# Attention's hash projections as fp32 products of the loaded rows, four quarters of the array in one call

## The chip, the cores and the metric

The kernel runs on one core of one Trainium2 chip. The metric is the device time of one execution in microseconds. Before the change the median of three runs is 671.51 us (669.77 to 671.78).

## What is computed

Three layers follow each other: bucketed attention, a mixture of experts with a capacity, and a second mixture of experts with a skip. The change touches the attention alone. Its reference, cut to what matters:

```python
q_bits = (np.einsum('bhsd,dk->bhsk', q, proj) > 0)
k_bits = (np.einsum('bhsd,dk->bhsk', k, proj) > 0)
mask = q_bucket[:, :, :, None] == k_bucket[:, :, None, :]
scores = np.where(mask, scale * np.matmul(q, k.transpose(0, 1, 3, 2)), -1000000000.0)
```

Batch 2, 8 heads, 768 positions, head dimension 64, 6 hash bits. Everything is float32.

## The kernel before, in words

**Units.** Attention is cut into 16 units of work: a batch, a pair of heads and one half of the 768 query positions. Each unit has six score tiles of 128 queries by 768 keys, one in each of six *slots*. There are 16 groups of keys, one for each batch and head; a unit uses two groups, and the first eight units use each pair of groups twice.

**How a score is made.** The loaded rows hold each head's 64 dimensions twice, on partitions 0 to 63 and 64 to 127 (qT and kT are laid out so). `splitq` and `splitk` (lines 143 to 158) cut them into a high part in fp32r and a rest: `Q1` and `K1` of 128 partitions, `Q2` and `K2` of 76. The score is the sum of two fp32r products (lines 199 and 201). Partitions 64 to 75 of `Q2` and `K2` hold the hash: 12 rows, six bits and six complements, 0 or 1 for queries and 0 or -BIG for keys, so that a pair in different buckets falls far below.

**The projections.** These 12 rows are what `projq` and `projk` make (lines 170 to 185): products of the signed projection matrix with the split rows, two fp32r products for each block of 384 positions (lines 172 and 173 for queries, 181 and 182 for keys), into a PSUM tile, and an eviction by VectorE that compares with a threshold (lines 175 and 184). `project` (line 160) does one or two of them in one PSUM tile `aux`, of which there is one buffer, shared with `fin`; where it does two, the second is put into partitions 32 to 43 by a projection matrix with 32 columns of zeros in front. There are 32 query and 32 key projections. The matrix is split in `signs` (line 72).

**The order.** Everything is issued in an order written out by hand, lines 327 to 445. For each slot (u, i) the kernel issues the score and its row maximum (VectorE, lines 203 to 205), the splits that are planned for the slot, at slot 1 the loads for later units, two products of attention and values (`av`, line 235, fp32, one head in each half of the columns), steps of the router's counting (`gens`, from unit 9 on), the projections planned for the slot (line 389), transposes of an older exponential (line 221), and the exponential of this slot on ScalarE (line 212). At slot 0 of unit 3 and later come the three products `fin` of a unit three before (line 278). The plan: query projections of the next unit at slots 2 and 3, those of a first K group at slots 4 and 5, those of a second K group at slot 5 and at slot 1 of the next unit. Units 0 to 4 and 9 split one K group each, units 5 to 8 two, units 10 to 15 none. Loads of kT, qT and v are issued from SP's queue; kT has three buffers, qT four. Scores have two PSUM buffers, so a score waits for the exponential two slots before.

**Start.** Before the first slot the kernel loads, splits group 0 and the first query block, projects them, then splits group 1 and the second query block (lines 331 to 342).

**After attention** come the two mixtures. At line 1248 their router makes four fp32 products of 192 columns, each with 32 columns of the array, side by side in one PSUM tile; the code before the change has no product that sets 64 rows of the array against the other 64.

```python
nc.tensor.matmul(s4[32 * d:32 * d + 32, :], self.wsg[:, d, :], yT[:, d, :],
                 start=True, stop=True, tile_position=(0, 32 * d))
```

Of the kernel before, what the change touches and what calls it, by code (L numbers as in the profile page):

```python
# [7 lines left out]
F32 = mybir.dt.float32  # L8
F32R = mybir.dt.float32r
# [4 lines left out]
ALU = mybir.AluOpType  # L14
# [4 lines left out]
BIG = 2.0 ** 33  # L19
# [4 lines left out]
class Net:  # L24
# [17 lines left out]
    def consts(self):  # L42
        nc = self.nc
        c = self.c = self.ctx.enter_context(self.pool("consts", 1))

        self.rows = ExitStack()
        x = self.x = self.rows.enter_context(self.pool("xp", 1))
        self.warm = x.tile([1, 1], F32, name="warm")
        nc.vector.memset(self.warm, 0.0)
        nc.scalar.activation(self.warm, self.warm, AF.Exp)  # L50
        self.zero = c.tile([128, 256], BF, name="zero")
        nc.vector.memset(self.zero, 0.0)
        jp = self.jp = x.tile([128, 128], I32, name="jp")
        nc.gpsimd.iota(jp, pattern=[[1, 128]], base=0, channel_multiplier=-1)

        ri = x.tile([12, 1], I32, name="ri")
        nc.gpsimd.iota(ri, pattern=[[0, 1]], base=0, channel_multiplier=1)
        thr = self.thr = x.tile([12, 2], F32, name="thr")
        nc.vector.tensor_scalar(thr[:, 0:1], ri, 5.5, -TINY, op0=ALU.is_gt, op1=ALU.mult)
        nc.vector.tensor_scalar(thr[:, 1:2], ri, 5.5, -TINY, op0=ALU.is_lt, op1=ALU.mult)  # L60

        sg = x.tile([128, 2, 12], F32, name="sg")
        nc.vector.memset(sg[:, 0, 0:6], 1.0)
        nc.vector.memset(sg[:, 0, 6:12], -1.0)
        nc.vector.memset(sg[:, 1, 0:6], -1.0)
        nc.vector.memset(sg[:, 1, 6:12], 1.0)

        prs = x.tile([128, 2, 76], F32, name="prs")
        nc.vector.memset(prs, 0.0)
        self.sg, self.prs = sg, prs  # L70

    def signs(self):

        nc, x, sg, prs = self.nc, self.x, self.sg, self.prs
        pr = x.tile([128, 12], F32, name="pr")
        nc.sync.dma_start(pr, self.A["proj"])
        nc.vector.tensor_tensor(prs[:, :, 32:44], sg, pr[:, None, :].to_broadcast([128, 2, 12]), op=ALU.mult)
        ph = x.tile([128, 2, 76], F32R, name="ph")
        nc.vector.tensor_copy(ph, prs)
        pl = x.tile([128, 2, 76], F32R, name="pl")  # L80
        nc.vector.tensor_tensor(pl, prs, ph.bitcast(F32), op=ALU.subtract)

        pk = x.tile([128, 76], F32R, name="pk")
        nc.vector.tensor_copy(pk[0:64], prs[0:64, 1, :])
        nc.vector.tensor_tensor(pk[64:128], prs[64:128, 1, :], ph[64:128, 1, :].bitcast(F32), op=ALU.subtract)
        self.ph, self.pl, self.pk = ph, pl, pk

    def ident(self):
        self.idf = self.c.tile([128, 128], F32, name="idf")
# [14 lines left out]
    def attention(self, r, later):  # L104

        nc, A = self.nc, self.A
        with self.rows as ctx:
# [44 lines left out]
            def splitq(u, a, eng=nc.gpsimd, ceng=nc.vector):  # L152
                d = UD[u]
                Q1 = d["Q1", a] = st.tile([128, 384], F32R, name="Q1")
                Q2 = d["Q2", a] = st.tile([76, 384], F32R, name="Q2")
                copy(ceng, Q1, d["q", a])
                eng.tensor_tensor(Q1[64:128], d["q", a][64:128], Q1[64:128].bitcast(F32), op=ALU.subtract)  # L157
                copy(ceng, Q2[0:64], d["q", a][0:64])

            def project(fs, tag="aux"):  # L160

                p = ps.tile([44, 384], F32, name="aux", tag=tag, bufs=1 if tag == "aux" else 2)

                k = len(fs)
                gs = [f(x, y, p[0:12 + 32 * i], slice(32 - 32 * i, 44), (i == k - 1, True)) for i, (f, x, y) in enumerate(fs)][::-1]
                for _ in range(2):
                    for g in gs:
                        next(g)

            def projq(u, a, p, c, ends):  # L170
                d = UD[u]
                nc.tensor.matmul(p, self.ph[:, 0, c], d["Q1", a], start=ends[0], stop=False, skip_group_check=True)
                nc.tensor.matmul(p, self.pl[:, 0, c], d["Q1", a], start=False, stop=ends[1], skip_group_check=True)
                yield
                nc.vector.tensor_scalar(d["Q2", a][64:76], p[32 - c.start:44 - c.start], self.thr[:, 0:1], None, op0=ALU.is_gt)
                yield

            def projk(g, j, p, c, ends):
                d = KH[g]
                sl = slice(j * 384, (j + 1) * 384)  # L180
                nc.tensor.matmul(p, self.pk[:, c], d["K1"][:, sl], start=ends[0], stop=False, skip_group_check=True)
                nc.tensor.matmul(p, self.ph[0:64, 1, c], d["K2"][0:64, sl], start=False, stop=ends[1], skip_group_check=True)
                yield
                nc.vector.tensor_scalar(d["K2"][64:76, sl], p[32 - c.start:44 - c.start], self.thr[:, 1:2], -BIG, op0=ALU.is_gt, op1=ALU.mult)
                yield

            def score(u, i):
# [148 lines left out]
            splitq(0, 0, nc.vector, nc.scalar)  # L336
            for g in range(2):
                loadv(g)
            project([(projk, 0, 0), (projk, 0, 1)], "pT")
            project([(projq, 0, 0)])  # L340
            splitk(1, nc.gpsimd, nc.scalar)
            splitq(0, 1, nc.vector, nc.scalar)
            loadk(order[0])
            loadv(order[0])
            loadq(1)
# [2 lines left out]
            for u in range(NU):  # L348
                if u + 1 < NU:
                    for a in range(2):  # L350
                        splits.setdefault((u, a), []).append((splitq, u + 1, a))
                        projs.setdefault((u, 2 + a), []).append((projq, u + 1, a))
                for x, g in enumerate(kplan.get(u, [])):
                    splits.setdefault((u, 2 + x), []).append((splitk, g))
                    for j in range(2):
                        at = (u, 4 + j) if x == 0 else ((u, 5), (u + 1, 1))[j]
                        projs.setdefault(at, []).append((projk, g, j))
            gens, full = [], [None]
            setup = {(0, 2): self.ident, (1, 3): self.consts2, (2, 3): later, (4, 3): r.consts2}
            projs[0, 0] = [(projk, 1, 0)]  # L360
            projs[0, 1] = [(projk, 1, 1)]
            projs[0, 2].append((projq, 0, 1))
            for u in range(NU):
                for i in range(6):
                    g = u * 6 + i
                    score(u, i)
                    if (u, i) in setup:
                        setup[u, i]()
                    for f, *x in splits.get((u, i), []):
                        f(*x, ceng=nc.scalar if u == 0 else nc.vector)  # L370
                    if i == 1:
                        if u + 2 < NU:
                            loadq(u + 2)
                        for _ in kplan.get(u + 1, []):
                            if nload < len(order):
                                loadk(order[nload])
                                loadv(order[nload])
                                nload += 1
                    ua, ca = (u - 1, i - 4) if i >= 4 else (u - 2, i + 2)
                    if ua >= 0:  # L380
                        av(ua, ca)

                    if i and gens and (i == 1 or u == NU - 1 or not full[0]):
                        full[0] = next(gens[0], self)
                        if full[0] is self:
                            gens.pop(0)
                            full[0] = None
                    if (u, i) in projs:
                        project(projs[u, i])

                    gp = g - 4 if g % 2 == 0 else g - 5
                    if gp >= 0:
                        tu, ti = divmod(gp, 6)
                        for cp in ((0, 1) if g % 2 == 0 else (2,)):
                            tpose(tu, ti // 2, cp)
                            if cp == 0:
                                expo(u, i)
                    if gp < 0 or g % 2:
                        expo(u, i)
                    if i == 0 and u >= 3:  # L400
                        fin(u - 3)
                        if u - 3 in (6, 7, 11):
                            q = 3 * (6, 7, 11).index(u - 3)
                            gens.append(r.count0(q, q + 3, sm, ps, ("pT", 2, "aux")))
# [1317 lines left out]
```

## Time and profile before

| | |
|---|---|
| median of three runs | 671.51 us |
| lowest and highest | 669.77, 671.78 us |
| profiled execution | 671.69 us |
| its span in the trace | 669.9 us |
| mean granted TensorE clock | 0.957 of full speed |
| TensorE busy | 621.7 us, 93% of the span |
| VectorE busy | 489.5 us, 73% |
| ScalarE busy | 398.9 us, 60% |
| GpSimd busy | 159.2 us, 24% |

All durations below come from the one profiled execution, whose time lies 0.2 us above the median. PE is TensorE, PEld its weight loads, DVE is VectorE, ACT is ScalarE, POOL is GpSimd, SP is the engine whose queue issues most loads. "L181" is line 181 of the kernel. Matmuls are pipelined: the duration of one contains latency that lies beside the next, so the cost of a matmul to the engine is read from one start to the next start. "busy tenths" and PEclk are given for 40 equal slices of the span, each about 16.7 us.

### The profile page before, as it was taken

How to read it: one execution, taken by the hardware profiler on the slowest of the kernel's cores; microseconds unless marked ns; L12 is line 12 of the kernel's file. 1: busy time of each engine (PE TensorE's matmuls, PEld its weight loads, DVE VectorE, ACT ScalarE, POOL GpSimd, SP SyncE). 2: the span in 40 equal slices, each digit the busy share in tenths (PEclk: the TensorE clock that was granted, in tenths of full speed). 3: DMA queues.
4: the chain of work that ended last, by engine and by line, in shares of the span. 5: the costliest groups of instructions: out<-in, count | busy, mean ns of one | idle time of the engine just before them, and what ended most of it. 6: DMA issues, size and time to landing. Idle time of an engine off the chain costs nothing.

```text
span 669.9 us, 11398 instructions
## 1 busy us (share of the span) xinstructions
PE 621.7 (93%) x3781; PEld 435.4 (65%) x3781; DVE 489.5 (73%) x1547; ACT 398.9 (60%) x909; POOL 159.2 (24%) x212
## 2 busy tenths in 40 slices
PE   7999999999999999956888899999999999999992
PEld 4666566655566666745747586686787778777781
DVE  7887788888877777475858776867633567999981
ACT  5677766666577777521525555554554557987870
POOL 2244233333111110142012130321502322211200
PEclk7799999999999999958988999999999999999996
DMA  6215212222111010035357828557665379999600
GB/s 199 96 38 160 74 41 79 89 92 72 48 63 34 0 49 2 2 132 193 127 157 292 253 53 281 169 174 256 217 219 191 111 263 363 388 381 326 231 22 13
DMA packets 53239, 99.69 MB, mean 149 GB/s; under 512 B 6421, under 2 KB 12949, under 8 KB 53168
## 3 DMA queue, kind: packets, MB, share of 16 engines
q1 hardware_dynamic: 42016, 76.21, 34.0%
q10 hardware_dynamic: 7072, 13.63, 5.9%
q0 software_dynamic: 4080, 8.99, 4.1%
q8 instruction: 34, 0.56, 0.3%
q14 instruction: 37, 0.30, 0.1%
HBM read 88.72 MB, written 12.46 MB: 151 GB/s over the span
## 4 chain that ended last, share of the span: by engine, by line
PE 73%; DVE 16%; DMA 3%; issue 3%; ACT 2%; POOL 1%; SPq 0%; ACTq 0%; POOLq 0%; DVEq 0%
PE av L235 10%; PE ph L1172 10%; PE pT L221 10%; PE y L1197 6%; PE S L201 5%; PE S L199 4%; DVE wlo L1359 4%; PE y L1203 4%; PE py L1419 2%; PE ph L1417 2%; PE ph L1419 2%; PE py L1418 2%; PE ph L1418 2%; PE py L1417 2%; PE fin L278 1%
## 5 line engine op out<-in xcount | busy, mean ns | idle before, releaser
L1359 DVE TENSOR_TENSOR wlo<-w,whi 128x512 fp32r<-128x512 f32 x192 | 123.6, 685 | 25.2 <-ACT whi L1358 22.8
L224 ACT ACTIVATE PT<-pT 128x512 f32<-128x512 f32 x135 | 80.3, 596 | 70.9 <-PE pT L221 70.8
L203 DVE TENSOR_REDUCE nm<-S 128x1 f32<-128x768 f32 x96 | 91.9, 957 | 31.3 <-PE S L201 29.1
L1358 ACT ACTIVATE whi<-w 128x512 fp32r<-128x512 f32 x192 | 109.4, 622 | 0.4 <-issue 0.4
L1172 PE MATMUL ph<-xT,w 128*128 128x192 f32 x512 | 104.8, 349 | 4.2 <-PEq L1517 4.2
L212 ACT ACTIVATE P<-S,b,g 128x768 f32<-128x768 f32 x96 | 94.8, 987 | 6.4 <-DVE b L205 6.4
L1172 PEld LDWEIGHTS ph<-xT,w 128*128 128x128 f32 x512 | 85.4, 198 | 14.4 <-issue 9.7
L221 PE MATMUL pT<-idf,P 128*128 128x128 f32 x576 | 83.3, 281 | 0.4 <-ACT PT L227 0.3
L221 PEld LDWEIGHTS pT<-idf,P 128*128 128x128 f32 x576 | 64.4, 142 | 29.4 <-issue 17.5
L235 PE MATMUL av<-PT,vd 128*64 128x384 f32 x360 | 77.5, 511 | 0.0
L157 POOL TENSOR_TENSOR Q<-qd,Q 64x384 fp32r<-64x384 f32 x30 | 31.1, 1038 | 144.3 <-PE pT L221 87.4
L199 PE MATMUL S<-K,Q 128*128 128x512 f32 x192 | 59.2, 390 | 0.7 <-ACT P L212 0.5
L1177 ACT ACTIVATE h<-ph 128x128 f32<-128x128 f32 x64 | 17.7, 277 | 61.2 <-PE ph L1172 34.2
L201 PE MATMUL S<-K,Q 76*128 76x512 f32 x192 | 51.5, 350 | 0.7 <-ACT Q L139 0.7
L201 PEld LDWEIGHTS S<-K,Q 76*128 76x128 f32 x192 | 30.6, 196 | 6.0 <-ACT K L139 1.2
L150 POOL TENSOR_TENSOR K<-kd,K 64x768 fp32r<-64x768 f32 x15 | 27.3, 1822 | 26.1 <-DVE K L141 12.2
L1203 PE MATMUL y<-w,h 128*64 128x512 f32 x128 | 32.9, 620 | 0.0
L235 PEld LDWEIGHTS av<-PT,vd 128*64 128x64 f32 x360 | 18.0, 134 | 22.7 <-issue 19.2
L199 PEld LDWEIGHTS S<-K,Q 128*128 128x128 f32 x192 | 30.8, 199 | 2.5 <-ACT P L212 1.7
L1320 POOL DMA_INDIRECT tb<-rec,ii x16 | 16.7, 1043 | 65.0 <-DVE cnt L1317 47.9
L1419 PE MATMUL py<-whi,hl 128*128 128x512 f32 x72 | 29.3, 406 | 1.4 <-DVE hl L1428 1.4
L1417 PE MATMUL py<-whi,hh 128*128 128x512 f32 x72 | 29.9, 416 | 0.0
(383 smaller groups left out, 1129.4 us busy)
## 6 DMA issues: line engine op xcount, KB each, us to landing
w<-w SPq DMA_DIRECT2D x28, 1024.0 KB
w<-u SPq DMA_DIRECT2D x26, 1024.0 KB
kd<-kT SPq DMA_DIRECT2D x16, 384.0 KB
qd<-qT SPq DMA_DIRECT2D x32, 192.0 KB
w<-u ACTq DMA_DIRECT2D x6, 1024.0 KB
w<-w ACTq DMA_DIRECT2D x4, 1024.0 KB
xd<-X SPq DMA_DIRECT2D x4, 780.0 KB
vd<-v SPq DMA_DIRECT2D x16, 192.0 KB
```

Source lines behind the costliest of these rows:

```text
L199: nc.tensor.matmul(S[:, n0:n1], d["Q1", a][:, ts], kd["K1"][:, n0:n1], start=True, stop=False)
L201: nc.tensor.matmul(S[:, n0:n1], d["Q2", a][:, ts], kd["K2"][:, n0:n1], start=False, stop=True)
L203: nc.vector.tensor_reduce(d["nm"][:, c], S, op=ALU.max, axis=AX.X, negate=True)
L212: nc.scalar.activation(P, S, AF.Exp, bias=d["b"][:, c], scale=d["g"][:, c], accum_out=d["s"][:, c])
L221: nc.tensor.transpose(p[:, a, b, :], d["P"][2 * ip + b][:, (2 * cp + a) * 128:(2 * cp + a + 1) * 128], self.idf)
L224: nc.scalar.activation(dst, p.rearrange("p a b q -> p a (b q)"), AF.Copy)
L235: nc.tensor.matmul(d["av"][64 * a:64 * a + 64, :], VH[b * 8 + 2 * p + a][:, c, :], d["PT"][:, c, a * 384:(a + 1) * 384], start=(c == 0), s ...
L1172: nc.tensor.matmul(ph, w1[f // 4][:, d, f % 4 * 128:f % 4 * 128 + 128], xT[:, d, :], start=(d == 0), stop=(d == 3))
L1203: nc.tensor.matmul(y2[64 * h:64 * h + 64, :], h2[:, 4 * h + f, :], res["w2"][h][:, f, :], start=(f == 0), stop=(f == 3))
L1358: nc.scalar.activation(hi[:, c, :], w[:, c, :], AF.Copy)
L1359: nc.vector.tensor_tensor(lo[:, c, :], w[:, c, :], hi[:, c, :].bitcast(F32), op=ALU.subtract)
L1417: nc.tensor.matmul(out, a[0][:, i, :], hi[:, i % 4, :], start=start, stop=False)
```

## The change

The signed projection matrix is no longer split; it stays in fp32 with 12 columns for queries and 12 for keys. Each projection is one fp32 product of it with the loaded rows (`d["q", a]` and `d["k"]`, not their splits). Product i of a call uses 64 rows of the array, the lower or the upper half in turn, and the 32 columns from 32 i, and writes PSUM partitions 32 i to 32 i + 11. A call takes up to four products; the evictions of the first two follow it, those of the other two come in the next slot. The plan is other: both query projections of the next unit and both of a first K group are one call at slot 3; both of a second K group are one call at slot 1 of the next unit; group 1 is one call at slot 0 of unit 0. Before the first slot, the second query block is split ahead of the projections, and all four projections of group 0 and unit 0 are one call.

```diff
--- before.py
+++ after.py
@@ -64,26 +64,15 @@
         nc.vector.memset(sg[:, 0, 6:12], -1.0)
         nc.vector.memset(sg[:, 1, 0:6], -1.0)
         nc.vector.memset(sg[:, 1, 6:12], 1.0)
-
-        prs = x.tile([128, 2, 76], F32, name="prs")
-        nc.vector.memset(prs, 0.0)
-        self.sg, self.prs = sg, prs
+        self.sg = sg
 
     def signs(self):
 
-        nc, x, sg, prs = self.nc, self.x, self.sg, self.prs
+        nc, x = self.nc, self.x
         pr = x.tile([128, 12], F32, name="pr")
         nc.sync.dma_start(pr, self.A["proj"])
-        nc.vector.tensor_tensor(prs[:, :, 32:44], sg, pr[:, None, :].to_broadcast([128, 2, 12]), op=ALU.mult)
-        ph = x.tile([128, 2, 76], F32R, name="ph")
-        nc.vector.tensor_copy(ph, prs)
-        pl = x.tile([128, 2, 76], F32R, name="pl")
-        nc.vector.tensor_tensor(pl, prs, ph.bitcast(F32), op=ALU.subtract)
-
-        pk = x.tile([128, 76], F32R, name="pk")
-        nc.vector.tensor_copy(pk[0:64], prs[0:64, 1, :])
-        nc.vector.tensor_tensor(pk[64:128], prs[64:128, 1, :], ph[64:128, 1, :].bitcast(F32), op=ALU.subtract)
-        self.ph, self.pl, self.pk = ph, pl, pk
+        self.prs = x.tile([128, 2, 12], F32, name="prs")
+        nc.vector.tensor_tensor(self.prs, self.sg, pr[:, None, :].to_broadcast([128, 2, 12]), op=ALU.mult)
 
     def ident(self):
         self.idf = self.c.tile([128, 128], F32, name="idf")
@@ -159,29 +148,32 @@
 
             def project(fs, tag="aux"):
 
-                p = ps.tile([44, 384], F32, name="aux", tag=tag, bufs=1 if tag == "aux" else 2)
-
-                k = len(fs)
-                gs = [f(x, y, p[0:12 + 32 * i], slice(32 - 32 * i, 44), (i == k - 1, True)) for i, (f, x, y) in enumerate(fs)][::-1]
-                for _ in range(2):
-                    for g in gs:
-                        next(g)
-
-            def projq(u, a, p, c, ends):
+                p = ps.tile([128, 384], F32, name="aux", tag=tag, bufs=1 if tag == "aux" else 2)
+                gs = [f(x, y, p[32 * i:32 * i + 12], i) for i, (f, x, y) in enumerate(fs)]
+                for g in gs:
+                    next(g)
+                for i, g in enumerate(gs):
+                    next(g)
+                    if i == 1:
+                        yield
+
+            def quarter(p, i, which, a):
+                r = 64 * (i % 2)
+                nc.tensor.matmul(p, self.prs[r:r + 64, which, :], a[r:r + 64], start=True, stop=True, tile_position=(r, 32 * i))
+
+            def projq(u, a, p, i):
                 d = UD[u]
-                nc.tensor.matmul(p, self.ph[:, 0, c], d["Q1", a], start=ends[0], stop=False, skip_group_check=True)
-                nc.tensor.matmul(p, self.pl[:, 0, c], d["Q1", a], start=False, stop=ends[1], skip_group_check=True)
+                quarter(p, i, 0, d["q", a])
                 yield
-                nc.vector.tensor_scalar(d["Q2", a][64:76], p[32 - c.start:44 - c.start], self.thr[:, 0:1], None, op0=ALU.is_gt)
+                nc.vector.tensor_scalar(d["Q2", a][64:76], p, self.thr[:, 0:1], None, op0=ALU.is_gt)
                 yield
 
-            def projk(g, j, p, c, ends):
+            def projk(g, j, p, i):
                 d = KH[g]
                 sl = slice(j * 384, (j + 1) * 384)
-                nc.tensor.matmul(p, self.pk[:, c], d["K1"][:, sl], start=ends[0], stop=False, skip_group_check=True)
-                nc.tensor.matmul(p, self.ph[0:64, 1, c], d["K2"][0:64, sl], start=False, stop=ends[1], skip_group_check=True)
+                quarter(p, i, 1, d["k"][:, sl])
                 yield
-                nc.vector.tensor_scalar(d["K2"][64:76, sl], p[32 - c.start:44 - c.start], self.thr[:, 1:2], -BIG, op0=ALU.is_gt, op1=ALU.mult)
+                nc.vector.tensor_scalar(d["K2"][64:76, sl], p, self.thr[:, 1:2], -BIG, op0=ALU.is_gt, op1=ALU.mult)
                 yield
 
             def score(u, i):
@@ -336,10 +328,10 @@
             splitq(0, 0, nc.vector, nc.scalar)
             for g in range(2):
                 loadv(g)
-            project([(projk, 0, 0), (projk, 0, 1)], "pT")
-            project([(projq, 0, 0)])
+            splitq(0, 1, nc.vector, nc.scalar)
+            for _ in project([(projk, 0, 0), (projk, 0, 1), (projq, 0, 0), (projq, 0, 1)]):
+                pass
             splitk(1, nc.gpsimd, nc.scalar)
-            splitq(0, 1, nc.vector, nc.scalar)
             loadk(order[0])
             loadv(order[0])
             loadq(1)
@@ -349,17 +341,15 @@
                 if u + 1 < NU:
                     for a in range(2):
                         splits.setdefault((u, a), []).append((splitq, u + 1, a))
-                        projs.setdefault((u, 2 + a), []).append((projq, u + 1, a))
+                        projs.setdefault((u, 3), []).append((projq, u + 1, a))
                 for x, g in enumerate(kplan.get(u, [])):
                     splits.setdefault((u, 2 + x), []).append((splitk, g))
                     for j in range(2):
-                        at = (u, 4 + j) if x == 0 else ((u, 5), (u + 1, 1))[j]
-                        projs.setdefault(at, []).append((projk, g, j))
+                        projs.setdefault((u, 3) if x == 0 else (u + 1, 1), []).append((projk, g, j))
             gens, full = [], [None]
             setup = {(0, 2): self.ident, (1, 3): self.consts2, (2, 3): later, (4, 3): r.consts2}
-            projs[0, 0] = [(projk, 1, 0)]
-            projs[0, 1] = [(projk, 1, 1)]
-            projs[0, 2].append((projq, 0, 1))
+            projs[0, 0] = [(projk, 1, 0), (projk, 1, 1)]
+            left = None
             for u in range(NU):
                 for i in range(6):
                     g = u * 6 + i
@@ -385,8 +375,12 @@
                         if full[0] is self:
                             gens.pop(0)
                             full[0] = None
+                    if left:
+                        next(left, None)
+                        left = None
                     if (u, i) in projs:
-                        project(projs[u, i])
+                        left = project(projs[u, i])
+                        next(left, None)
 
                     gp = g - 4 if g % 2 == 0 else g - 5
                     if gp >= 0:
```

## Rows read from the trace of the kernel before

**Rows 1.** The page: busy time and share of TensorE; granted clock in 40 slices.

```profile
PE 621.7 (93%) x3781; PEld 435.4 (65%) x3781; DVE 489.5 (73%) x1547; ACT 398.9 (60%) x909; POOL 159.2 (24%) x212
...
PEclk7799999999999999958988999999999999999996
```

**Rows 2.** Busy time in two stretches: length, PE, PEld, DVE, ACT, POOL, clock, DMA.

```profile
0.00:20.00 20.00, 16.02 (x53) 9.20 (x54) 14.71 (x36) 10.77 (x20) 6.17 (x10) 0.69 0.69 224
120.00:160.00 40.00, 40.00 (x236) 23.63 (x234) 32.70 (x78) 25.66 (x52) 12.56 (x13) 1.00 0.19 58
```

**Rows 3.** The chain that ended last: `fin` at slot 0, start and duration.

```profile
58.08 0.74 PE fin L278 x6
74.34 0.74 PE fin L278 x6
...
142.32 0.74 PE fin L278 x6
159.71 0.74 PE fin L278 x6
178.44 0.74 PE fin L278 x6
194.51 0.74 PE fin L278 x6
209.69 0.74 PE fin L278 x6
```

**Rows 4.** Timeline of TensorE, 102 to 113 us: start, duration, line, operation.

```profile
103.21 0.37 PE L181 MATMUL aux<-K,pk 128*44 128x384 f32 x1
...
104.36 0.66 PE L221 MATMUL pT<-idf,P 128*128 128x128 f32 x4
...
109.71 0.34 PE L181 MATMUL aux<-K,pk 128*12 128x384 f32 x1
109.98 0.34 PE L182 MATMUL aux<-K,ph 64*12 64x384 f32 x1
110.25 0.66 PE L221 MATMUL pT<-idf,P 128*128 128x128 f32 x4
...
111.54 0.87 PE L235 MATMUL av<-PT,vd 128*64 128x384 f32 x4
112.34 0.35 PE L172 MATMUL aux<-Q,ph 128*12 128x384 f32 x1
...
112.70 0.49 PE L221 MATMUL pT<-idf,P 128*128 128x128 f32 x3
```

**Rows 5.** Timeline of TensorE at a router product, line 1248, and the next.

```profile
350.94 0.53 PE L1248 MATMUL s<-yT,wsg 128*32 128x192 f32 x8
351.41 0.59 PE L1172 MATMUL ph<-xT,w 128*128 128x192 f32 x2
```

**Rows 6.** Timeline of TensorE in unit 9; in brackets idle time and releaser.

```profile
168.80 0.34 PE L172 MATMUL aux<-Q,ph 128*12 128x384 f32 x1 [1.00 <-DVE Q L175]
```

**Rows 7.** Timeline of all engines at the start; first scores of units 0, 1, 2.

```profile
5.24 0.94 ACT L139 ACTIVATE Q<-qd 128x384 fp32r<-128x384 f32 x2 [0.30 <-DMA qd<-qT]
...
7.84 0.84 PE L199 MATMUL S<-K,Q 128*128 128x512 f32 x2
...
9.39 1.87 DVE L157 TENSOR_TENSOR Q<-qd,Q 64x384 fp32r<-64x384 f32 x1 [0.18 <-ACT Q L139]
...
11.29 0.96 DVE L203 TENSOR_REDUCE nm<-S 128x1 f32<-128x768 f32 x1
...
25.93 0.59 PE L199 MATMUL S<-K,Q 128*128 128x512 f32 x2
...
39.80 0.60 PE L199 MATMUL S<-K,Q 128*128 128x512 f32 x2
```

**Rows 8.** Groups by line and shape, 0 to 240 us: count, busy us, mean ns.

```profile
L184 DVE TENSOR_SCALAR K<-aux,thr 12x384 fp32r<-12x384 f32 x32 | 19.5, 608 | 3.6 <-PE aux L182 2.8
L175 DVE TENSOR_SCALAR Q<-aux,thr 12x384 fp32r<-12x384 f32 x30 | 18.2, 608 | 1.0
```

## The prediction

> **What bounds the kernel now.** First the busy shares of the page: TensorE is busy for 93% of the span, and its clock is at full speed in nearly every slice of the first 40% [rows 1]. An average says little, so next the table by stretch [rows 2]: from 120 to 160 us, in the middle of attention, TensorE is busy for all of the 40 us at a granted clock of 1.00 (2.4 GHz), VectorE for 32.70 and ScalarE for 25.66. In the first 20 us it is another picture: TensorE 16 of 20, clock 0.69. So attention has a start-up, where loads, VectorE and a slow clock count, and a long stretch in which TensorE's queue sets the pace. There a microsecond taken from TensorE is a microsecond of the span.
>
> The chain of waits gives the length of each unit, because every unit from the fourth on holds one group of `fin` products at the same place [rows 3]. A unit that prepares one K group lasts 74.34 - 58.08 = 16.26 us; one that carries the work of two, 159.71 - 142.32 = 17.39; one with queries alone, 209.69 - 194.51 = 15.18. The unit from 159.71 to 178.44 lasts 18.73 and is an exception, below.
>
> The timeline of TensorE gives the price of a projection as start to next start (durations hold latency that overlaps the next instruction) [rows 4]. One K projection, two instructions, goes from 109.71 to 110.25: 0.54. One Q projection, from 112.34 to 112.70: 0.36. Two K projections of different groups in one tile, from 103.21 to 104.36: 1.15. These account for the units: 15.18 + 2 x 0.54 = 16.26, and 15.18 + 0.54 + 1.15 + 0.54 = 17.41 (17.39 seen). A unit without any projection would be 15.18 - 2 x 0.36 = 14.46.
>
> **The change, part by part.** *New price of a call.* All projections of a slot become one call with two or four fp32 products, each two instructions on TensorE. Two rows bound it. The attention-value product `av` is two fp32 products of 384 columns in two column halves, four instructions: from 111.54 to 112.34, 0.80 [rows 4]. The router's product at line 1248 is four fp32 products of 192 columns in four column quarters, eight instructions: from 350.94 to 351.41, 0.47 [rows 5]. So four quarters do run beside each other, and a call of 384 columns should cost what `av` costs, 0.80, with two products or with four. I take 0.80: same columns, same two instructions for each product, same change of tile shape at the end. I give it no lower end, as no row has an fp32 product of 384 columns in less. What neither row shows is that the quarters also alternate between the upper and the lower 64 rows of the array. If nothing ran beside anything, `av`'s four instructions would take 1.60, so a call of two products 1.60 and of four 3.20. That is the upper end.
>
> *Steady units.* New lengths: queries alone 14.46 + 0.80 = 15.26; one K group, in the same call, also 15.26; with a second K group, a second call at slot 1 of the next unit, 16.06. Units 2, 3 and 4 (one group): 3 x (16.26 - 15.26) = 3.0 gained. Unit 5 had 14.46 + 0.72 + 0.54 + 1.15 = 16.87 and gets 15.26: 1.6. Units 6 to 8: 3 x (17.39 - 16.06) = 4.0. Units 10 to 14: 5 x 0.08 = 0.4 lost. Unit 15 projects nothing.
>
> *Unit 9.* By the prices it should last 14.46 + 0.72 + 0.54 + 1.08 = 16.80, and lasts 18.73; 1.9 us are lost to VectorE, which has the counting steps in its queue. One us of that is TensorE waiting, at the second Q projection, for the eviction of the first out of the one PSUM buffer [rows 6]. In one call that wait has no place. I take 16.06 + 0.9 = 17.0: 1.7 gained, with ends of 0.7 (all 1.9 stay) and 2.7 (none).
>
> *Start-up.* VectorE loses the five splits and the clearing of the signs. The first query's companion is split before the first projection, so that its VectorE subtraction, which takes 1.87 us behind the first evictions now, comes before them. ScalarE has the first query block at 5.24, the second one lands soon after on the same queue. I expect the first reduction about 1.2 us earlier than 11.29. From the first score at 7.84 to unit 2 at 39.80, six K and five Q projections (6 x 0.54 + 5 x 0.36 = 5.0 at full clock) become calls at three places (2.4): at most 2.6 more, some of it behind VectorE and ScalarE [rows 7]. I take 2.5 in all, ends 1.0 and 3.8.
>
> *What costs nothing.* The evictions stay 64 of 608 ns [rows 8], only in pairs: two behind the call, two a slot later. Cover: VectorE is busy 32.70 of 40 us, or 14.2 of a 17.39 us unit, and the same work must fit into 16.06 (88%). If that cover goes, the next score's reduction is late, then its exponential, then the score two slots on, which wants its buffer. Queued behind a waiting pair is that reduction alone; its score ends later than the call, so the wait should not show. The POOL subtractions no longer stand ahead of a projection; only scores wait for them. SP's loads of kT: the buffer of a group is now held until its product, up to 4 slots (some 10 us) after its split. The load that waits for it, and the v and q loads behind that, are wanted about seven slots (19 us) on; if the cover went, a K split would be late. TensorE's instruction count is unchanged (128 before, 64 x 2 after).
>
> *Sum.* 3.0 + 1.6 + 4.0 + 1.7 - 0.4 + 2.5 = 12.4 us. What follows attention is the same work and should move as one. The profiled execution took 671.69 us (span 669.9), 0.2 over the median of 671.51. So 671.69 - 12.4 = 659.3, or 659.2 against the median.
>
> **The rivals.** *The row halves exclude each other (slower).* All four products write one PSUM tile, from two halves of the array's rows, in alternation, in the order written. If a product in the other half must wait, everything is serial, at 3.20 and 1.60. Units: one group 17.66 (+1.4, three times), unit 5 +0.8, units 6 to 8 19.26 (+1.9 each), unit 9 +0.5, five units of queries +0.9 each: 15.5 us, and no start-up gain: 687. It turns from gain to loss where a call costs, on average, more than 0.80 + 9.9 / 17 = 1.4 (17 steady calls). For it: no row of the trace has two row halves at work at once. Against it: the quarters of line 1248 share a tile too and overlap [rows 5], though they use all rows. The Trainium skill, "TensorEngine Tiling (Array Packing)", section "Restrictions and Gotchas", speaks for this rival: it says that different row tiles cannot access one PSUM bank at the same time. By that rule the time is the 687; no run here shows it so far. I weigh it low because the quarters write different partitions. Chance 0.10.
>
> *Half of the overlap (no change).* Only products of the same row half run beside each other, so every call costs 1.60. One group 16.06 (-0.2 each), unit 5 -0.8, units 6 to 8 17.66 (+0.3 each), unit 9 -0.1, queries alone +0.9 each: +3.7, less some 2 of the start-up: 673. The order of issue alternates halves, which speaks against it. Chance 0.05.
>
> *VectorE takes over (smaller gain).* Evictions in pairs delay reductions and units 5 to 9 keep their length: 1.6 + 4.0 + 1.7 = 7.3 of the gain goes, 666.5. For it: unit 9 does it already; against: 88% is not full. Chance 0.07.
>
> **How the numbers follow.** The forecast has 0.78. Its own range is 656 to 662.5 (start-up -1.3 to +1.5, unit 9 +-1, one us between runs). With the third rival, 655.5 to 666.5 holds some 0.82. A measurement of this kernel can tell 0.3%, or 2 us. Faster: 0.78 + 0.07 = 0.85; slower: 0.10 and a little of the second rival, 0.11; the rest, 0.04, the same.
>
> **What would show it.** Eight instructions of a call starting within 0.4 us of each other and the next product 0.8 us after the first; `fin` groups 15.3 us apart with one K group and 16.1 with two; TensorE still busy throughout 60 to 160 us; no wait of TensorE for an eviction in unit 9. Wrong: calls of 1.6 or 3.2 us, units longer than 16.3, TensorE idle behind VectorE with units unchanged, or a gain in attention given back after 285 us.

## The result, and the profile after

The changed kernel takes 660.64 us (median of four runs, 659.53 to 661.93) against 671.64 for the kernel before on the same chips: a ratio of 0.984, with a 95% interval of 0.9808 to 0.9871. That is 11.0 us, faster as forecast and 1.4 us above the predicted 659.2. The profiled execution has a span of 658.0 us.

The page after the change and two stretches of the table by stretch (columns as in [rows 2]):

```profile
PE 606.6 (92%) x3781; PEld 423.1 (64%) x3781; DVE 487.5 (74%) x1542; ACT 400.1 (61%) x909; POOL 157.9 (24%) x212
...
PEclk8899999999999999958989999999999999999996
```

```profile
0.00:20.00 20.00, 14.23 (x57) 7.18 (x57) 12.38 (x32) 10.76 (x20) 6.10 (x10) 0.79 0.53 177
120.00:160.00 40.00, 39.86 (x256) 23.16 (x255) 36.14 (x87) 27.93 (x54) 15.22 (x15) 1.00 0.28 85
```

TensorE lost 15.1 us of busy time with the same 3781 instructions, and in the middle of attention it is still busy for 39.86 of 40 us. VectorE had 32.70 there before [rows 2] and now has 36.14, but the stretch is not the same work: since the units moved forward, it now takes in 10 us of unit 9. Unit 7 alone, in the same view, had VectorE busy for 14.24 of 17.40 us (124.76 to 142.16) and now has 14.35 of 16.08 (117.60 to 133.68), 89%: nearly the same work in less time.

One call of four products, in the timeline of TensorE (unit 3, slot 3):

```profile
62.45 0.50 PE L162 MATMUL aux<-qd,prs 64*12 64x384 f32 x2
62.47 0.50 PE L162 MATMUL aux<-kd,prs 64*12 64x384 f32 x2
62.78 0.49 PE L162 MATMUL aux<-qd,prs 64*12 64x384 f32 x2
62.80 0.49 PE L162 MATMUL aux<-kd,prs 64*12 64x384 f32 x2
63.22 0.66 PE L213 MATMUL pT<-idf,P 128*128 128x128 f32 x4
```

A call of two products (unit 11):

```profile
190.79 0.82 PE L162 MATMUL aux<-qd,prs 64*12 64x384 f32 x4
191.54 0.66 PE L213 MATMUL pT<-idf,P 128*128 128x128 f32 x4
```

Of the eight instructions of the call of four, the first four start within 0.02 us, the other four 0.33 us later, and the transposes start 63.22 - 62.45 = 0.77 us after the call. The call of two takes 191.54 - 190.79 = 0.75. That stands against 0.54 for one K and 0.36 for one Q projection [rows 4].

The `fin` groups, which mark the units [rows 3], in the timeline of TensorE:

```profile
55.51 0.90 PE L270 MATMUL fin<-R,OT 128*128 128x144 f32 x6
70.84 0.90 PE L270 MATMUL fin<-R,OT 128*128 128x144 f32 x6
...
133.68 0.90 PE L270 MATMUL fin<-R,OT 128*128 128x144 f32 x6
...
149.77 0.90 PE L270 MATMUL fin<-R,OT 128*128 128x144 f32 x6
...
167.62 0.90 PE L270 MATMUL fin<-R,OT 128*128 128x144 f32 x6
...
183.85 0.90 PE L270 MATMUL fin<-R,OT 128*128 128x144 f32 x6
...
199.17 0.90 PE L270 MATMUL fin<-R,OT 128*128 128x144 f32 x6
```

A unit with one K group lasts 70.84 - 55.51 = 15.33 us, one with two 149.77 - 133.68 = 16.09, one of queries alone 199.17 - 183.85 = 15.32. Unit 9 (from 149.77) lasts 17.85 and unit 14 (from 230.48 to 247.08) 16.60.

Read from the same timeline, the units of all thirteen traces look so (us; "fin of 3" and "fin of 15" are the starts of these groups, "rest" is the span after the second; the kernels below "before, again" are those of the experiments):

```
kernel           fin of 3  units 3, 4    unit 5  6 to 8  unit 9  unit 13  unit 14  fin of 15   rest
before              57.92  16.26 16.34   16.85   17.39   18.73   15.18    15.90     256.46   413.4
before, again       56.37  16.26 16.32   16.86   17.39   18.72   15.18    15.86     254.88   413.3
changed             55.51  15.33 15.34   15.33   16.09   17.85   15.32    16.60     247.08   410.9
e0_again            54.96  15.33 15.34   15.33   16.09   17.84   15.32    16.60     246.51   414.5
e1_lower_rows       55.19  15.33 15.34   15.33   16.08   17.85   15.31    16.60     246.67   412.0
e2_all_rows         55.35  15.34 15.34   15.34   16.09   17.85   15.32    16.60     246.96   414.0
e3_one_by_one       62.39  17.55 17.55   17.54   18.93   19.64   15.95    16.62     273.48   414.6
e4_old_products     66.97  16.82 16.83   16.82   17.96   18.45   15.26    16.52     268.90   411.5
e5_old_plan         61.29  17.59 17.59   17.59   18.34   19.31   16.08    16.49     270.72   411.9
e6_start            55.37  15.33 15.33   15.34   16.09   17.85   15.33    16.60     246.94   415.3
e7_counting         54.77  15.34 15.77   16.07   16.09   16.74   15.31    16.00     245.81   414.2
e9_counting2        54.99  15.33 15.34   15.33   16.09   16.75   15.32    16.00     244.85   412.3
e10_all             53.27  15.33 15.33   15.34   16.09   16.75   15.32    16.00     243.13   413.9
```

Units repeat to some hundredths of a us, the start varies by 0.6 to 1.6 us between two executions of one kernel, and the rest by 4.4 us over all kernels. So the attention part of the gain is, as means of two traces each, 255.67 - 246.80 = 8.9 us, of which 198.54 - 191.57 = 7.0 lie in units 3 to 14. What a pair of executions shows beyond that is the rest: the first two traces differ by 11.9 us in span, and 2.5 of it lie in their rests. The attention part alone would be a ratio of 0.987, the upper end of the interval of the medians.

The granted clock of the start differs too. Up to the `fin` of unit 3 its mean is 0.85 and 1.00 in the two traces before, 0.91 and 0.88 in the two of the changed kernel. So the first pair (57.92 against 55.51, 2.4 us) has the higher clock on the side of the change, the second pair (56.37 against 54.96, 1.4 us) on the side of the kernel before; what the start gave at a like clock is not shown.

### The profile page after: what moved, and what is told of

The parts are those of the page before. It is cut to its first block, busy times and chain, and to the rows that moved or that the text cites. A ratio compares the mean times of both kernels' runs of the same rounds, so it can differ in the third digit from the quotient of the medians.

```text
span 658.0 us, 11405 instructions
## 1 busy us (share of the span) xinstructions
PE 606.6 (92%) x3781; PEld 423.1 (64%) x3781; DVE 487.5 (74%) x1542; ACT 400.1 (61%) x909; POOL 157.9 (24%) x212
## 4 chain that ended last, share of the span: by engine, by line
PE 66%; DVE 19%; issue 5%; DMA 4%; ACT 3%; POOL 2%; SPq 0%; ACTq 0%; POOLq 0%; DVEq 0%
PE av L227 10%; PE pT L213 9%; PE ph L1166 8%; PE y L1191 5%; PE S L191 5%; DVE wlo L1353 5%; PE S L193 5%; PE y L1197 3%; DMA xg<-xd,idsb 2%; DVE nm L195 2%; PE py L1413 2%; PE ph L1411 2%; PE ph L1413 2%; PE py L1412 2%; PE aux L162 2%
## 5 line engine op out<-in xcount | busy, mean ns | idle before, releaser
L1166 PE MATMUL ph<-xT,w 128*128 128x192 f32 x512 | 102.9, 345 | 3.8 <-PEq L1511 3.8
L213 PEld LDWEIGHTS pT<-idf,P 128*128 128x128 f32 x576 | 62.2, 141 | 51.4 <-issue 30.7
```

The source lines that it names most:

```text
L213: nc.tensor.transpose(p[:, a, b, :], d["P"][2 * ip + b][:, (2 * cp + a) * 128:(2 * cp + a + 1) * 128], self.idf)
L1166: nc.tensor.matmul(ph, w1[f // 4][:, d, f % 4 * 128:f % 4 * 128 + 128], xT[:, d, :], start=(d == 0), stop=(d == 3))
```

## The experiments

**The kernels themselves, again.** No edit. 

> The changed kernel again, unaltered, for a second trace. Theory (attention gave 9.4 us, the other 2.5 us between the two profiled executions are a matter of the stage after it, where the clock fell to half between 380 and 390 us before and not after): the last fin at 247.1 again, the rest of the span anywhere from 411 to 414 us. Rival (the change makes the stage after attention shorter): last fin at 247.1 and 410.9 us after it again.

> The kernel before, unaltered, for a second trace. Theory: units as in the first trace to 0.02 us, last fin at 256 to 257, and again 411 to 415 us after it. Rival (the stage after attention is longer before the change): 413.4 us or more after it.

Measured: 414.5 us after the last `fin` for the changed kernel, 413.3 for the one before, against 410.9 and 413.4 in the first traces. The rival, that the change shortens the later stage, falls: over the eight traces with the new products in the new plan (all but the first two and the three numbered e3 to e5) the rest is 413.4 in the mean. What makes the rest vary is not settled. In the traces with 413.4, 414.5 and 413.3 the granted clock falls in five-microsecond stretches between 370 and 390 us (to 0.80, 0.64 and 0.50), and in the one with 410.9 it stays at 1.00; but it also falls, to 0.66, in the one with 412.3. The clock is a candidate, not a cause that is shown.

**Row halves.** The two edits of `quarter`, and what was expected of each:

```diff
-                r = 64 * (i % 2)
+                r = 0
```

> All products of a call use the lower 64 rows of the array; the four column quarters stay. Theory (column quarters overlap, row halves play no part): a call still goes from its first product to the next transpose in 0.77 us, units of 15.3 and 16.1 us, 660 to 662 us in all. Rival (the alternation of row halves is what lets neighbours overlap): a call of four takes 1.5 to 2.6 us, 672 to 682 us.

```diff
-                nc.tensor.matmul(p, self.prs[r:r + 64, which, :], a[r:r + 64], start=True, stop=True, tile_position=(r, 32 * i))
+                nc.tensor.matmul(p, self.prs[:, which, :], a, start=True, stop=True, tile_position=(0, 32 * i))
```

> Each product uses all 128 rows, which hold the 64 dimensions twice, so the projection is doubled and its sign is the same; column quarters stay. Theory: 0.77 us for a call, 660 to 662 us. Rival (64-row tiles cost or gain a change of tile shape): a call of 0.6 to 0.7 or 0.9 to 1.0 us, 657 to 659 or 663 to 666 us.

Measured: 660.45 and 662.78 us. The same call in the timeline of TensorE, first with the lower rows, then with all rows:

```profile
62.13 0.50 PE L162 MATMUL aux<-qd,prs 64*12 64x384 f32 x2
...
62.90 0.66 PE L213 MATMUL pT<-idf,P 128*128 128x128 f32 x4
```

```profile
62.30 0.50 PE L161 MATMUL aux<-qd,prs 128*12 128x384 f32 x2
...
63.07 0.66 PE L212 MATMUL pT<-idf,P 128*128 128x128 f32 x4
```

0.77 us in both, and units as in the changed kernel to 0.02. The 2.3 us between the two times, one execution each, are their rests (412.0 and 414.0) and starts. The column quarters do the work; which rows they use, and whether they alternate, is free here.

**One product after the other.** The matrix is padded with 96 columns of zeros; product i covers columns 0 to 32 i + 11 and adds into the tile. It uses all 128 rows, so the projection is doubled and its sign is kept.

```diff
-                nc.tensor.matmul(p, self.prs[r:r + 64, which, :], a[r:r + 64], start=True, stop=True, tile_position=(r, 32 * i))
+                nc.tensor.matmul(p[0:32 * i + 12], self.prs[:, which, 96 - 32 * i:108], a, start=ends[0], stop=ends[1], skip_group_check=True)
```

> Plan and fp32 products of the change, but every product covers all columns from the first (matrix padded with zeros) and adds into one tile, so none can run beside another. The three fin products (432 columns in all) take 0.65 us, so 384 columns take 0.58. Theory (the gain is the overlap): a call of four 2.3 to 2.5 us, of two 1.2, so 8 x 1.6 + 9 x 0.45 = 17 us more in the units and some 3 in the start: 677 to 682 us. Rival (the gain comes from fewer calls, fewer waits for the one PSUM buffer and no splits ahead): 660 to 664 us.

Measured: 689.94 us. A call of four in the timeline of TensorE:

```profile
86.89 1.54 PE L163 MATMUL aux<-kd,prs 128*108 128x384 f32 x4
88.36 1.59 PE L163 MATMUL aux<-qd,prs 128*44 128x384 f32 x4
89.87 0.65 PE L214 MATMUL pT<-idf,P 128*128 128x128 f32 x4
```

89.87 - 86.89 = 2.98 us, 0.75 for each product; the expectation, scaled from `fin`, had 0.58, and the time lies 8 us above its upper end. Units with one K group are 2.2 us longer, the start 7. The plan without the overlap is 22 us slower than the kernel before (667.68, measured beside it, one execution each); the rival falls.

**Old products in the new plan.** The two fp32r products on the split rows, four projections in one tile with up to 108 zero-padded columns.

```diff
-                quarter(p, i, 0, d["q", a])
+                c, o = slice(96 - 32 * i, 108), p[0:32 * i + 12]
+                nc.tensor.matmul(o, self.ph[:, 0, c], d["Q1", a], start=ends[0], stop=False, skip_group_check=True)
+                nc.tensor.matmul(o, self.pl[:, 0, c], d["Q1", a], start=False, stop=ends[1], skip_group_check=True)
```

(and the same for K with `pk` and `ph`)

> Plan of the change (one call a slot), but the old two fp32r products on the split rows, in up to 108 zero-padded columns. Theory (the products give the gain): a call of four costs 2 x 0.36 + 2 x 0.54 and a little for the padding, 1.8 to 2.0 us against 0.77, one of two K 1.15, one of two Q as before: 8 x 1.1 + 4 x 0.4 = 10 us more, 670 to 673 us, about the time before. Rival (the plan gives the gain): 660 to 664 us.

Measured: 682.21 us, 9 above the upper end of the expectation. A call of four in the timeline of TensorE, and one that waits in the start:

```profile
90.74 0.43 PE L184 MATMUL aux<-K,pk 128*108 128x384 f32 x1
...
93.04 0.60 PE L224 MATMUL pT<-idf,P 128*128 128x128 f32 x4
```

```profile
38.65 0.65 PE L185 MATMUL aux<-K,ph 64*108 64x384 f32 x1 [1.45 <-POOL K L149]
```

The call costs 93.04 - 90.74 = 2.30 where 1.8 to 2.0 was expected. A unit with one K group lasts 16.82, where the old plan had 16.26 and the new products 15.33; units 3 to 14 together are 201.93 - 191.57 = 10.4 us longer than in the changed kernel. So in the units the theory holds: the products give the gain. The rest is the start: unit 3 begins at 66.97, 11.5 us later than in the first trace of the changed kernel. With the old products a call at slot 3 stands behind GpSimd's split of slot 2, and TensorE waits for it in order, but all such waits of the start add up to 2.1 us. Up to unit 3 TensorE's idle time grows from 7.9 to 9.7 us and its busy time from 47.6 to 57.3, at a mean granted clock of 0.80 instead of 0.91. How much of that the dearer calls make and how much the clock is not separated. What this run shows of the plan is that it does not pay with the old products; that their inputs also come too late for it is shown for 2.1 us.

**New products in the old plan.**

```diff
-                        projs.setdefault((u, 3), []).append((projq, u + 1, a))
+                        projs.setdefault((u, 2 + a), []).append((projq, u + 1, a))
...
-                        projs.setdefault((u, 3) if x == 0 else (u + 1, 1), []).append((projk, g, j))
+                        projs.setdefault((u, 4 + j) if x == 0 else ((u, 5), (u + 1, 1))[j], []).append((projk, g, j))
```

> The new products in the old plan: query projections at slots 2 and 3, key projections at slots 4, 5 and 1, mostly one product in a call. Theory (a call costs 0.77 us however many products it holds): units of queries alone 16.1, with one K group 17.6, with two 18.4: about 2.3 us more in eight units and 0.8 in five, 22 us, 680 to 684 us, slower than before the change. Rival (one fp32 product on 64 rows is itself cheaper than two fp32r products): 655 to 664 us.

Measured: 684.39 us against 671.0 for the kernel before beside it, and units of 16.08, 17.59 and 18.34, each within 0.06 of the expectation. A call of a single product in the timeline of TensorE:

```profile
86.58 0.81 PE L162 MATMUL aux<-qd,prs 64*12 64x384 f32 x2
87.33 0.66 PE L213 MATMUL pT<-idf,P 128*128 128x128 f32 x4
```

0.75 us for one, 0.75 for two and 0.77 for four. One alone is dearer than what it replaces (0.54 and 0.36); the gain is made only by sharing. The three runs together: products without the plan, plan without the products, and both without the overlap are all slower than the kernel before, by 13 to 22 us.

**The start.**

```diff
-            splitq(0, 1, nc.vector, nc.scalar)
-            for _ in project([(projk, 0, 0), (projk, 0, 1), (projq, 0, 0), (projq, 0, 1)]):
+            for _ in project([(projk, 0, 0), (projk, 0, 1), (projq, 0, 0)]):
                 pass
             splitk(1, nc.gpsimd, nc.scalar)
+            splitq(0, 1, nc.vector, nc.scalar)
...
-            projs[0, 0] = [(projk, 1, 0), (projk, 1, 1)]
+            projs[0, 0] = [(projk, 1, 0), (projk, 1, 1), (projq, 0, 1)]
```

> Only the start: the second query block is split after the first projections, as before the change, and its projection joins the call of slot 0. Theory (the first call waits for a query block that lands 2 us after the first, and the evictions with it): first row maximum at 9.5 to 10.0 us where the changed kernel has 11.06, unit 3 some 1 us earlier, 659 to 660 us. Rival (the start is bound further on by ScalarE's copies and exponentials): first maximum earlier, unit 3 not, 660.6 us.

Measured: 662.88 us (0.987, interval 0.9825 to 0.9924), unit 3 at 55.37. The first maximum did not come earlier. VectorE's timeline shows the exchange:

```profile
9.13 1.88 DVE L146 TENSOR_TENSOR Q<-qd,Q 64x384 fp32r<-64x384 f32 x1 [0.59 <-ACT Q L128]
11.04 0.96 DVE L195 TENSOR_REDUCE nm<-S 128x1 f32<-128x768 f32 x1
```

The evictions were done by 8.54, but the query split stood ahead of the maximum in VectorE's queue again, as in the kernel before, and beside GpSimd's K split (8.77 to 10.60) it took 1.88 us where it takes 0.56 alone. A wait was traded for a collision; both the theory and the rival had the first maximum earlier.

**Unit 9 and unit 14.** First with the second K groups one unit earlier, then with unit 9's split alone moved; both move unit 14's query call to slot 1.

```diff
-            kplan = {0: [2], 1: [3], 2: [4], 3: [5], 4: [6], 5: [7, 8], 6: [9, 10], 7: [11, 12], 8: [13, 14], 9: [15]}
+            kplan = {0: [2], 1: [3], 2: [4], 3: [5], 4: [6, 7], 5: [8, 9], 6: [10, 11], 7: [12, 13], 8: [14, 15]}
...
-                        projs.setdefault((u, 3), []).append((projq, u + 1, a))
+                        projs.setdefault((u, 1 if u == 14 else 3), []).append((projq, u + 1, a))
```

> The second K groups come one unit earlier (units 4 to 8 have two, unit 9 none), and unit 14's query call moves from slot 3 to slot 1. Theory (units 9 and 14 are held up by VectorE, which has counting steps and paired evictions in the same slots, and one counting step that collides with POOL's split): unit 9 falls from 17.85 to 16.1 to 16.6, unit 14 from 16.60 to 15.9 to 16.1, one call more (0.77) in unit 4 to 8: 0.8 to 1.5 us gained, 659 to 660 us. Rival (those units wait for something else): both keep their length, and the call more makes 661.4 us.

```diff
-                    splits.setdefault((u, 2 + x), []).append((splitk, g))
+                    splits.setdefault((u, 1 if u == 9 else 2 + x), []).append((splitk, g))
```

> Unit 9's split of its last K group moves from slot 2 to slot 1, out of the counting step's slot, and unit 14's query call from slot 3 to slot 1; no call more. Theory (in unit 9 VectorE's 24-element step waits out GpSimd's split, 1.64 us, in unit 14 evictions pair with counting steps): unit 9 16.2 to 16.8 instead of 17.85, unit 14 16.0 instead of 16.60, 1.6 to 2.2 us off attention, 658.5 to 659.5 us. Rival (VectorE's load in unit 9, not the collision, is the limit): unit 9 17.5 to 17.85, about 660 us.

Measured: 662.49 us (0.988, 0.9835 to 0.9926) and 659.51 (0.987, 0.9839 to 0.9909). The times can't tell these from the changed kernel; the units can. Unit 9 falls from 17.85 to 16.74 and 16.75, unit 14 from 16.60 to 16.00. In the first the extra call takes 0.43 in unit 4 and 0.74 in unit 5 back, so that units 3 to 14 gain 0.5 us, less than expected; in the second they gain 1.7, as expected. The changed kernel's unit 9, GpSimd and VectorE, then the score that came late; and the same VectorE step where the split was moved:

```profile
156.56 1.82 POOL L139 TENSOR_TENSOR K<-kd,K 64x768 fp32r<-64x768 f32 x1 [2.30 <-DVE K L130]
156.61 1.82 DVE L551 TENSOR_TENSOR baq<-baq,rW 128x24 f32<-128x24 f32 x1
...
163.79 0.99 ACT L204 ACTIVATE P<-S,b,g 128x768 f32<-128x768 f32 x1 [1.51 <-DVE b L197]
...
165.02 0.59 PE L191 MATMUL S<-K,Q 128*128 128x512 f32 x2 [0.85 <-ACT P L204]
```

```profile
156.13 0.18 DVE L551 TENSOR_TENSOR baq<-baq,rW 128x24 f32<-128x24 f32 x1
```

A step of 0.18 us began 0.05 us after GpSimd's split and ended 0.05 us after it, and VectorE's lag reached TensorE by way of the exponential. In unit 14 it is the other pairing, counting steps and evictions ahead of a maximum:

```profile
238.98 1.51 DVE L580 TENSOR_SCALAR gn<-mrow,m 128x1152 bf16<-128x1152 f32 x2
240.52 1.25 DVE L168 TENSOR_SCALAR Q<-aux,thr 12x384 fp32r<-12x384 f32 x2
241.80 0.96 DVE L195 TENSOR_REDUCE nm<-S 128x1 f32<-128x768 f32 x1
```

**All of it.** The edit that moved unit 9's split and unit 14's call, and in the start: the second query block is split in slot 0 by GpSimd instead of before the first slot, its projection joins the call of slot 0, and the splits issued in unit 0 come one slot later. The lines on the start, cut:

```diff
-            splitq(0, 1, nc.vector, nc.scalar)
...
-                        splits.setdefault((u, a), []).append((splitq, u + 1, a))
+                        splits.setdefault((u, a + (u == 0)), []).append((splitq, u + 1, a))
...
+            splits[0, 0] = [(splitq, 0, 1)]
```

> The same, and the start: the second query block is split in slot 0 by GpSimd behind the first maximum, its projection joins the call of slot 0, and unit 0's own splits move one slot later, so that the first exponential does not queue on ScalarE behind copies of a query block that lands at 11.4. Theory (the start waits for these two in-order queues): first maximum at 9.5 to 10.2, first exponential by 11 instead of 13.15, unit 3 at 53.5 to 54.5 instead of 55.0 to 55.5, 657 to 658.5 us. Rival (VectorE's work from 10 to 40 us is the limit of the start): first exponential earlier, unit 3 at 55, 659 us.

Measured: 656.82 us (median of six, 655.9 to 658.8), 0.9818 of the kernel before (669.36 in this comparison) with an interval of 0.9794 to 0.9843. Unit 3 starts at 53.27, and the first maximum and exponential are early, in the timeline of VectorE and ScalarE:

```profile
9.24 0.96 DVE L195 TENSOR_REDUCE nm<-S 128x1 f32<-128x768 f32 x1 [0.77 <-PE S L193]
...
10.85 0.99 ACT L204 ACTIVATE P<-S,b,g 128x768 f32<-128x768 f32 x1 [1.18 <-DVE b L197]
```

The maximum starts 1.8 us earlier than in the changed kernel (11.06) and the exponential 2.3 (13.15): what stood ahead of them in the in-order queues of VectorE and ScalarE had held them. Unit 3 starts 1.5 us earlier than in any other trace here; the mean granted clock up to there, 0.90, is no higher than the 0.91 of the changed kernel's first trace. It is one trace, and starts of one kernel differ by 0.6 to 1.6, so the size is less sure than the direction. This kernel has the lowest time of the study; its interval still overlaps that of the changed kernel (0.9808 to 0.9871).

## Why the prediction was right, and where its sum was off

**The price of a call** was right: 0.80 forecast from `av` and the router's quarters, 0.75 measured with two products and 0.77 with four. The choice of the nearest row over the upper ends of 1.60 and 3.20 decided the case; the run without overlap, 2.98 for four, shows that the upper end was real.

**The rival of the row halves** falls. Before the change no row had two halves at work at once; after it they start 0.02 us apart in one PSUM tile, and the same call with one half or with all rows costs the same 0.77. The Trainium skill, "TensorEngine Tiling (Array Packing)", section "Restrictions and Gotchas", from which this rival had its support, does not agree with these traces for products in different column quarters. **Half of the overlap** falls by the same rows. In the sums of these two rivals unit 9 is not treated alike: its 0.9 us of VectorE's lag stands in the second (14.46 + 3.20 + 0.9) and not in the first (14.46 + 4.80), so one of the two is 0.9 us off; nothing hung on it.

**The units** came as forecast, a little too short: 15.33 for 15.26 and 16.09 for 16.06. The base of 14.46 was the mis-sized term: by the call's 0.77 it is 15.33 - 0.77 = 14.56. The prediction took off 2 x 0.36 for the Q projections, but in the trace before, the transposes behind a Q projection went faster (four from 115.51 to the score at 115.87, 0.36, against 0.41 from 110.25 [rows 4] to 110.66 behind a K projection), so removing one gave 0.05 less; two make the 0.10.

```profile
110.66 0.60 PE L199 MATMUL S<-K,Q 128*128 128x512 f32 x2
...
115.51 0.60 PE L221 MATMUL pT<-idf,P 128*128 128x128 f32 x4
115.87 0.60 PE L199 MATMUL S<-K,Q 128*128 128x512 f32 x2
```

Units 3 to 8 gained 7.4 against 7.6 forecast; units 10 to 13 lost 0.14 to 0.16 each instead of 0.08.

**Unit 9** gained 0.88 where 1.7 was taken, with 0.7 and 2.7 as ends. The wait for the eviction went, as said, but VectorE's lag stayed; moving the split out of the counting step's slot took 1.1 us of it away. **Unit 14** was costed at 0.08 lost and lost 0.70. There the step "the wait should not show" failed, and the third rival, VectorE, was right in these two; in units 5 to 8, which made up most of its price, it was not.

**The start** failed most: with unit 2 it was to give 3.5 us by unit 3 and gave 57.92 - 55.51 = 2.4 in the first pair of traces and 1.4 in the second. The maximum moved from 11.29 [rows 7] to 11.06 instead of to 10.1. The step "the second one lands soon after on the same queue" was wrong, as rows of the changed kernel's start show:

```profile
7.31 0.81 PE L162 MATMUL aux<-qd,prs 64*12 64x384 f32 x2 [1.00 <-DMA qd<-qT]
7.84 0.56 DVE L146 TENSOR_TENSOR Q<-qd,Q 64x384 fp32r<-64x384 f32 x1 [1.26 <-ACT Q L128]
...
8.43 1.23 DVE L176 TENSOR_SCALAR K<-aux,thr 12x384 fp32r<-12x384 f32 x2
...
9.68 1.27 DVE L168 TENSOR_SCALAR Q<-aux,thr 12x384 fp32r<-12x384 f32 x2
...
10.44 0.59 PE L193 MATMUL S<-K,Q 76*128 76x512 f32 x2 [1.77 <-DVE Q L168]
...
11.06 0.96 DVE L195 TENSOR_REDUCE nm<-S 128x1 f32<-128x768 f32 x1
...
11.38 0.94 ACT L128 ACTIVATE Q<-qd 128x384 fp32r<-128x384 f32 x2 [2.21 <-DMA qd<-qT]
...
13.15 0.99 ACT L204 ACTIVATE P<-S,b,g 128x768 f32<-128x768 f32 x1 [0.83 <-DVE b L197]
```

The second block landed at 7.3, 1.8 us after ScalarE began on the first (5.48). Three of the four products had started between 5.25 and 5.50, but the fourth waited for the block, and on VectorE all four evictions stood behind the block's split, which began at 7.84. They ran from 8.43 to 10.95, and the maximum behind them. The prediction's other half came true: the split itself took 0.56 us instead of 1.87. The 1.87 of the kernel before [rows 7] was a collision with GpSimd's K split (9.03 to 10.84), which the prediction did not see; so moving the split back in the run on the start brought the collision back. A small slip beside it: VectorE lost five instructions (1547 to 1542), four splits and the clearing, not five splits and the clearing.

**The sum.** Attention gave 8.9 us against 12.4: 7.4 in units 3 to 8, 0.9 in unit 9, 1.9 by unit 3 (3.5 forecast), less 1.3 in units 10 to 14 (0.4 forecast). The mechanism held in the steady units; in the start, unit 9 and unit 14 the gain was forecast too large. That the medians, 11.0 apart, lie closer to the forecast than the parts do is luck: they hold the rest of the program, which varies by more than the difference.

## What to carry to other kernels

Products that use few columns cost nearly the same alone as four abreast (0.75 and 0.77 us), so they pay only where the plan can gather them into one call; count calls, not products. To gather them, their inputs must be there early: here the raw loaded rows were, while for the split ones TensorE waited 2.1 us in the start. When the bound engine gets faster, look at the units where another engine already had an exceptional load, and read repeating units from the trace instead of the total time when the rest of the program varies.

## What the runs showed of the hardware that was not expected

A VectorE step that begins while GpSimd's K split runs can be held until the split is over: 0.18 us became 1.82, and 0.56 became 1.88; they ended 0.05 and 0.4 us after GpSimd's instruction, which took 1.82 and 1.83 us beside them and 1.80 in the changed kernel's start. Not every step is held: the maximum that began at 61.77 us beside the split of 61.14 to 62.96 took its usual 0.96. The rows fit what the Trainium skill states in "SBUF — State Buffer", section "Terms": that the two engines share a pair of ports which one instruction holds to its end. Of the eight instructions of a call, the first of all four products start together and the second of all four together, 0.33 us later, though the kernel issues the products one behind the other.
